# Dynamic convolution and a two-way maxout layer on one core: a new order of the 1024 inner units, a load in longer rows, and one softmax step in another place

## The chip, the cores and the metric

The kernel runs on one core of one Trainium2 chip. The metric is the device time of one execution in microseconds (us). A core has a matrix engine (TensorE, PE in the profile, with its weight loads shown apart as PEld), a vector engine (VectorE, DVE), an activation engine (ScalarE, ACT), a general engine (GpSimd, POOL) that in this kernel mostly issues DMAs, and SyncE (SP), which only issues DMAs. Each engine takes its own instructions in order and waits where one of them needs what another engine or a DMA has not yet finished.

## What is computed

Two layers follow each other, cut here to what matters:

```python
# x: [8, 4160, 192], weight_gen: [8, 4160, 8 heads, 7 taps]
w = softmax(weight_gen, over the 7 taps)
y[b, s, h, g] = sum over k of w[b, s, h, k] * x_padded[b, s + k, h, g]   # 6 zero rows in front of each sequence
# y as 33280 rows of 192; w1, w2: [192, 1024], w_out: [1024, 192]
out = maximum(y @ w1, y @ w2) @ w_out
```

The order of the 1024 inner units does not matter to the result, as long as the columns of `w1` and `w2` and the rows of `w_out` are taken in the same order.

## The kernel before, in words

The 33280 rows lie on 128 partitions, 260 consecutive rows on each; a "column" is one row on every partition. Columns are handled in 17 batches of 16 (the last has 4). Batches 0 and 1 are cut into units of 4 columns, the later ones into units of 8: units 0 to 7, then 8 to 36. Columns 32 to 39 are unit 8, the first half of batch 2.

**Convolution (DVE and ACT).** For each batch ACT takes the exponentials (`exp_sum`, L135), DVE sums them over the taps (`red`, L147), ACT takes the logarithm (`ln`, L151), DVE subtracts it (`shift`, L156), and `weights` (L159 to L170) lets ACT write the softmax weights twice each in bf16 to `en_t`. `mul` (L182) multiplies the 7 taps on DVE, and `adds` (L198, L204, L207) sums them to `y_t`. From unit 8 on, a DMA transpose issued by SP (L216) brings `y_t` to the feature layout `yt`. For units 0 to 7, PE does the sum of the taps and the transposition at once (`sum_transpose`, L239 to L257): it multiplies the products by an identity matrix into a PSUM tile `yps`, and ACT copies that to `yt` (L255, "feature copy" below).

**Inner layer (PE and ACT).** The maximum is written as `y@w1 + relu(y@(w2 - w1))`. So the kernel keeps `wd = w2 - w1` for the inner products (`hid_tile`, L291 to L304, PSUM tiles `hdp` and later `hd`), ACT takes the ReLU to `rd_t` (`relu`, L309), and the product `w10 = w1 @ w_out` is computed once on the chip (L594 to L667), so that an output is `yt @ w10` (`out_first`, L351) plus `rd_t @ wo` (`out_hidden`, L339). The 1024 inner units are cut into 8 chunks of 128; `wo` has the rows of one chunk on the 128 partitions, so that chunk f lies at `wo[:, f*192:(f+1)*192]`. `evac` (L378 to L413) lets ACT copy finished outputs from the PSUM tile `op_ps` to `o_t` (L395, "eviction" below), and SP stores them (L407).

**Weights at the start.** `load_w` and its neighbours (L537 to L552) bring `w1` and `w2` as f32 to the staging tiles `ws0E`, `ws1E` (rows 0 to 127) and `ws0T`, `ws1T` (rows 128 to 191, each half of the columns on 64 partitions). ACT casts `w1` to bf16 in three copies of 512 columns (L578, L632, L633). `w_diff` (L579 to L589) is called twice: the first call subtracts on DVE (L582, then L587) and copies three pieces to other partitions on ACT; the second subtracts once (L582) and copies on DVE. `wo` comes by one DMA from POOL (L621), behind two loads of `x` and ahead of a third, with f32 in HBM and bf16 in SBUF.

**Order.** The order on each engine is that of the code; nothing is rescheduled. The first part (L512 to L693) is written out by hand: the transposition of unit 0, first inner products, `w_diff(1)`, and so on. From group 3 on (`GROUPS`, two columns of work each up to column 15, then three) `hidden` (L458 to L485) puts the steps of a group in order: inner products, `out_first`, ReLU, `relay` (an ACT no-operation that waits for `out_first` and that `out_second` waits for), the last inner products, the last ReLU, then `ahead`, then `out_second` with `evac`, then `between`, then `beside`. Dictionary `early` (L712) gives `between` for groups 3 to 7, and the call at L785 gives `ahead` for groups 4 and 5: `weights(2, 0)`, the softmax weights of columns 32 to 39, is in `ahead` of group 5. `op_ps` and `yps` share a ring of two PSUM buffers up to group 7, so that `op_ps` of group 6 takes the buffer of `op_ps` of group 5 once its eviction is done.

Of the kernel before, what the change touches and what calls it, by code (L numbers as in the profile page):

```python
# [13 lines left out]
ALU = mybir.AluOpType  # L14
# [3 lines left out]
def _sub(base: bass.AP, off: int, dims):  # L18
    ap = [list(base.ap[0])] + [[int(s), int(c)] for s, c in dims]
    return dataclasses.replace(base, offset=base.offset + off, ap=ap)  # L20
# [3 lines left out]
def kernel(  # L24
# [9 lines left out]
    nc = tc.nc  # L34

    B, S, D = x.shape
    H, K = weight_gen.shape[2], weight_gen.shape[3]
    F = moe_w1.shape[1]
    P = 128
    PAD = K - 1  # L40
    WGC = H * K
    FCH = F // P
    HF = F // 2
# [10 lines left out]
    def pieces(b):  # L54
        n = BATCHES[b][1]
        at, done = [], 0
        for w in (4, 4, 4, 4) if b < 2 else (8, 8) if n == 16 else (n,):
            at.append((done, w))
            done += w
        return at  # L60
# [76 lines left out]
    def part(b, i, of):  # L137

        n = BATCHES[b][1]
        h0, h1 = n * i // of * H, n * (i + 1) // of * H  # L140
        return slice(h0, h1), h0 * K, [[K, h1 - h0], [1, K]]
# [7 lines left out]
    def ln(b, i=0, of=1):  # L149
        s_t = s_ts[b][:, part(b, i, of)[0]]  # L150
        nc.scalar.activation(out=s_t, in_=s_t, func=AF.Ln)  # L151
# [7 lines left out]
    def weights(b, o):  # L159

        w = dict(pieces(b))[o]
        if b not in en_ts:
            en_ts[b] = pen.tile([P, 16 * WGC * 2], BF16, name="en_t", tag="en")
        J = 2 if w == 4 and b < 2 else 1
        N = w * H // J
        for j in range(J):
            nc.scalar.activation(  # L167
                out=_sub(en_ts[b], (o * WGC + j * N * K) * 2, [[2 * N, K], [2, N], [1, 2]]),
                in_=_sub(wg_ts[b], (o * H + j * N) * K, [[1, K], [K, N], [0, 2]]), func=AF.Exp,
            )  # L170
# [62 lines left out]
    def half(j):  # L233
        return slice(64 * j, 64 * j + 64)


    LEFT = (0, 1, 2, K - 1)

    def sum_transpose(u, taps=range(K)):  # L239

        b, o, n = UNITS[u]
        assert n == 4
        yps = ps["r" if "r" in ps else "o"].tile([P, 1024], FP32, name="yps", tag="op")
        for k in range(6):
            for t in taps:
                for r in range(2):
                    at = (K * o + t * n) * D + k * P
                    nc.tensor.matmul(  # L248
                        yps[:, r * 512 + k * 64:r * 512 + (k + 1) * 64],
                        lhsT=m_t[half(r), at:at + P], rhs=ident[half(r), half(r)],  # L250
                        start=(k == 0 and t == taps[0]), stop=(t == taps[-1]),
                        skip_group_check=True,
                    )
        yt = pyt.tile([P, 8 // 2 * 3 * P], BF16, name="yt", tag="yt")
        yt_of[u] = nc.scalar.copy(out=_sub(yt, 0, [[64, 2], [P, 6], [1, 64]]),  # L255
                                  in_=_sub(yps, 0, [[512, 2], [64, 6], [1, 64]]))
        yt_ts[u] = yt  # L257
# [112 lines left out]
    def relay(last):  # L370

        go = nc.scalar.nop()  # L372
        for mm in last:
            tc.add_manual_dep(go.ins, mm.ins.name, SYNC, reason="bank of the other half")
        return go
# [50 lines left out]
    OUTS, c = [[], [], []], 0  # L426
# [8 lines left out]
    def room(g):  # L435

        t0, n = GROUPS[g]
        if "c" in ps:
            ab = ps["ab"].tile([P, 2048], FP32, name="hd2", tag="ab")
            for t in range(t0, t0 + n - 1):  # L440
                hd_at[t] = ab, (t - t0) * 1024
            hd_at[t0 + n - 1] = ps["c"].tile([P, 1024], FP32, name="hd1", tag="c"), 0
        else:
            for t in range(t0, t0 + n):
                hd_at[t] = ps["h"].tile([P, 1024], FP32, name="hdp", tag="hd"), 0
        rd = prd.tile([P, 3 * 1024], BF16, name="rd_t", tag="rd")
        for t in range(t0, t0 + n):
            rd_at[t] = (rd, t - t0)
        return rd

    def out_room(now, tag=None):
        tag = tag or ("r" if "r" in ps else "o")
        w, name = {"ab": (2048, "ab"), "c": (1024, "c")}.get(tag, (1024, "op"))
        tile_ = ps[tag].tile([P, w], FP32, name="op_ps", tag=name)
        for c in now:
            op_at[c // 2] = tile_, (c - now[0]) // 2 * D

    def hidden(g, now=(), between=lambda: None, beside=lambda: None, ahead=lambda: None):  # L458


        t0, n = GROUPS[g]
        rd = room(g)
        for t in range(t0, t0 + n - 1):
            hid_tile(t)
        if now:
            out_room(now, "ab" if n == 1 and "ab" in ps else None)
            last = out_first(now)
        if len(now) > 2:
            relu(rd, t0, n - 1)
        else:  # L470
            for t in range(t0, t0 + n - 1):
                relu(rd, t, 1)
        if now:
            go = relay(last)
        hid_tile(t0 + n - 1)
        if len(now) > 2:
            beside()
        relu(rd, t0 + n - 1, 1)
        ahead()
        if now:  # L480
            out_second(now, go)
            evac(now[0] // 2, len(now) // 2)
        between()
        if len(now) <= 2:
            beside()  # L485
# [17 lines left out]
    wd = consts.tile([P, 3 * F], BF16, name="wd")  # L503
    wo = consts.tile([P, FCH * D], BF16, name="wo")
# [7 lines left out]
    with tc.tile_pool(name="pstage", bufs=1) as pstage:  # L512
        ident_f = pstage.tile([P, P], FP32, name="ident_f")
        xs = pstage.tile([P, (PAD + 8) * D], FP32, name="xs")
        ws = {(kind, wi): pstage.tile([P, w], FP32, name=f"ws{wi}{kind}")
              for kind, w in (("E", F), ("T", HF)) for wi in range(2)}
# [3 lines left out]
        for p0, p1 in ((1, 16), (16, P)):  # L520
            nc.sync.dma_start(
                out=xs[p0:p1, 0:PAD * D],
                in_=bass.AP(tensor=x.tensor, offset=(p0 * CPP - PAD) * D,
                            ap=[[CPP * D, p1 - p0], [1, PAD * D]]),
# [20 lines left out]
        for wi, wsrc in enumerate((moe_w1, moe_w2)):  # L545
            for h in range(2):
                nc.sync.dma_start(
                    out=ws["T", wi][half(h), :],
                    in_=bass.AP(tensor=wsrc.tensor, offset=P * F + h * HF, ap=[[F, 64], [1, HF]]),
# [20 lines left out]
        for o in (0, 4, 8, 12):  # L570
            weights(0, o)
        nc.vector.tensor_copy(out=xb_ts[0][:, PAD * D:(PAD + 4) * D],
                              in_=xs[:, PAD * D:(PAD + 4) * D])
        first_mul = mul(0, 0)
        w1 = {kind: pstage.tile([P, w], BF16, name="w1" + kind)
              for kind, w in (("E", F), ("T", HF))}

        nc.scalar.copy(out=w1["E"][:, 0:HF], in_=ws["E", 0][:, 0:HF])  # L578
        def w_diff(h, copy):  # L579

            c0 = slice(h * HF, (h + 1) * HF)
            nc.vector.tensor_tensor(out=wd[:, c0], in0=ws["E", 1][:, c0], in1=ws["E", 0][:, c0],  # L582
                                    op=ALU.subtract)
            copy(out=wd_at(1, 2, h, 0, HF), in_=wd[0:64, c0])
            copy(out=wd_at(0, 1, h, 0, HF), in_=wd[64:P, c0])
            if h == 0:
                nc.vector.tensor_tensor(out=wd[:, 2 * HF:3 * HF], in0=ws["T", 1], in1=ws["T", 0],  # L587
                                        op=ALU.subtract)
            copy(out=wd_at(1 - h, 1 + h, h, 0, HF), in_=wd[half(h), 2 * HF:3 * HF])  # L589


# [18 lines left out]
        def keep_warm(times):  # L610
# [8 lines left out]
        behind(first_mul, load_x(0, 8, 4))  # L619
        load_x(0, 12, 4)  # L620
        nc.gpsimd.dma_start(  # L621
            out=wo[:, :].rearrange("p (f d) -> p f d", d=D),
            in_=bass.AP(tensor=moe_w_out.tensor, offset=0, ap=[[D, P], [P * D, FCH], [1, D]]),
        )
        load_x(1, 0, 8)

# [2 lines left out]
        mul(0, 4)  # L629


        nc.scalar.copy(out=w1["T"], in_=ws["T", 0])  # L632
        nc.scalar.copy(out=w1["E"][:, HF:F], in_=ws["E", 0][:, HF:F])  # L633
        rd = room(0)
        hid_tile(0)
        relu(rd, 0, 1)
# [65 lines left out]
    def end_of_1():  # L702
# [8 lines left out]
    none = lambda: None  # L711
    early = {  # L712
        3: (none, rest_of_1),
        4: (lambda: (behind(relu_of[8], load_x(2, 0, 8, halo=False)), sum_transpose(4),
                     behind(yt_of[4], load_wg(4, nc.gpsimd))), end_of_1),
        5: (lambda: sum_transpose(5, LEFT), none),
        6: (lambda: (behind(relu_of[12], load_x(2, 8, 8)), weights(2, 8), ln(3), sum_transpose(6, LEFT)), none),
        7: (lambda: (behind(relu_of[14], load_x(3, 0, 8)), sum_transpose(7, LEFT)), none),
    }
# [60 lines left out]
    for g in range(4, len(GROUPS)):  # L780
        if GROUPS[g][1] == 3 and "c" not in ps:
            later_ps()
        tiles = [t for t in range(GROUPS[g][0], sum(GROUPS[g])) if t >= 16]
        if g in early:
            hidden(g, OUTS[g], early[g][0], ahead=lambda: {4: lambda: (weights(1, 12), ln(2)), 5: lambda: weights(2, 0)}.get(g, none)())  # L785
            early[g][1]()
            steps(g, tiles)
        else:
            hidden(g, OUTS[g], beside=lambda: steps(g, tiles))
# [30 lines left out]
```

## Time and profile before

| | |
|---|---|
| median of 5 runs | 411.57 us (411.0 to 413.79) |
| the profiled execution, its own time | 412.04 us |
| its span, first to last instruction | 410.3 us |
| granted TensorE clock in it | 0.999 |
| busy PE, DVE, ACT, POOL | 398.4, 374.7, 357.5, 73.3 us |
| DMA traffic | 65.68 MB, mean 160 GB/s |
| load of `wo`: 384 KB, issue to landing | 7.8 us |

The page gives each engine's busy time, then the span in 40 slices, the DMA queues, the chain of work that ended last (followed back from the last instruction to what released it), and the costliest groups of instructions. The timeline gives the instructions of an engine in order: start, duration, engine, line, operation, and in brackets the idle time before it and what ended that. [...]

### The profile page before, as it was taken

To read this page: it belongs to the slowest core of one execution; us is meant where nothing else is said; L and a number is where in the kernel's file an instruction comes from. 1 tells how busy PE (TensorE), PEld (TensorE's weight loads), DVE (VectorE), ACT (ScalarE), POOL (GpSimd) and SP (SyncE) were. 2 spreads that over 40 slices of the span, in tenths; PEclk is the share of its full clock that TensorE was granted. 3 is DMA by queue.
4 is the path that set the end of the run, shared out by engine and by line. 5 is a ranking of instruction groups with operands and counts; after the bars stand their busy time and mean duration, and the time that the engine had idled before them with its cause. 6 is when DMAs were issued, how large, how long until landed. Compare 5 with 4: busy or idle time off the path is not lost.

```text
span 410.3 us, 15992 instructions
## 1 busy us (share of the span) xinstructions
PE 398.4 (97%) x7350; PEld 317.0 (77%) x7350; DVE 374.7 (91%) x219; ACT 357.5 (87%) x424; POOL 73.3 (18%) x101
## 2 busy tenths in 40 slices
PE   7889999999999999999999999999999999999995
PEld 3679899677777877777787778777777777787795
DVE  5999999999999999999999999999999999999000
ACT  6898998989999998899988999988999989888771
POOL 0311103121211022222101222211122212110000
PEclk9999999999999999999999999999999999999999
DMA  8966577768667864974787497489548638744513
GB/s 240 237 145 182 101 147 160 182 150 180 147 104 209 207 137 98 257 165 88 215 174 174 92 252 186 74 201 241 112 103 244 166 59 248 150 89 69 223 61 136
DMA packets 60384, 65.68 MB, mean 160 GB/s; under 512 B 47615, under 2 KB 48511, under 8 KB 60318
## 3 DMA queue, kind: packets, MB, share of 16 engines
q1 hardware_dynamic: 51934, 40.54, 36.5%
q0 software_dynamic: 8240, 24.04, 29.3%
q8 instruction: 57, 0.93, 0.9%
q10 hardware_dynamic: 144, 0.10, 0.1%
q14 instruction: 9, 0.07, 0.1%
HBM read 35.96 MB, written 25.56 MB: 150 GB/s over the span
## 4 chain that ended last, share of the span: by engine, by line
PE 83%; ACT 11%; DMA 3%; issue 2%; DVE 0%; SPq 0%; ACTq 0%
PE op_ps L339 38%; PE hd L299 36%; PE op_ps L351 7%; ACT rd_t L309 6%; DMA xs<-in_x_dram 3%; ACT en_t L167 1%; PE hdp L299 1%; ACT o_t L395 1%; ACT yt L255 1%; ACT e_t L135 1%; PE yps L248 0%; PE pw L655 0%; ACT sum_t L151 0%; ACT w L666 0%; ACT wd L589 0%
## 5 line engine op out<-in xcount | busy, mean ns | idle before, releaser
L309 ACT ACTIVATE rd_t<-hd 128x1024 bf16<-128x1024 f32 (+1 forms) x206 | 234.6, 1189 | 27.7 <-PE hd L299 26.3
L339 PE MATMUL op_ps<-wo,rd_t 64*128 64x192 bf16 x4160 | 210.5, 243 | 0.1
L339 PEld LDWEIGHTS <-rd_t 64*128 64x128 bf16 x4160 | 180.8, 94 | 15.7 <-ACTq L372 0.3
L299 PE MATMUL hd<-yt,wd 64*128 64x512 bf16 (+1 forms) x1584 | 187.3, 360 | 1.2 <-ACT rd_t L309 1.2
L182 DVE TENSOR_TENSOR m_t<-xb_t,en_t 128x10752 bf16<-128x10752 bf16 (+1 forms) x37 | 187.5, 5071 | 0.4
L299 PEld LDWEIGHTS <-wd 64*128 64x128 bf16 x1776 | 94.1, 94 | 43.2 <-issue 3.0
L224 POOL CAST gate<-yt 128x1 f32<-128x1 bf16 x29 | 38.6, 1332 | 272.0 <-DMA yt<-y_t 272.0
L198 DVE TENSOR_TENSOR m_t<-m_t 128x4608 bf16<-128x4608 bf16 (+1 forms) x32 | 76.8, 2401 | 0.1
L395 ACT COPY o_t<-op_ps 128x384 f32<-128x384 f32 (+1 forms) x99 | 57.3, 591 | 14.0 <-PE op_ps L339 13.3
L351 PE MATMUL op_ps<-w,yt 64*128 64x192 bf16 x780 | 55.5, 243 | 1.0 <-ACT o_t L395 1.0
L351 PEld LDWEIGHTS <-yt 64*128 64x128 bf16 x780 | 38.4, 94 | 17.5 <-issue 2.1
L204 DVE TENSOR_TENSOR m_t<-m_t 128x3072 bf16<-128x3072 bf16 (+1 forms) x29 | 50.0, 1724 | 0.1
L167 ACT ACTIVATE en_t<-wg_t 128x896 bf16<-128x896 f32 (+2 forms) x45 | 35.4, 821 | 0.0
L207 DVE TENSOR_TENSOR y_t<-m_t 128x1536 bf16<-128x1536 bf16 (+1 forms) x29 | 27.3, 941 | 0.5
L385 DVE COPY o_last<-op_ps 128x192 f32<-128x192 f32 x1 | 0.4, 357 | 26.1 <-ACT o_last L385 26.1
L156 DVE TENSOR_TENSOR wg_t<-wg_t,sum_t 128x280 f32<-128x280 f32 (+5 forms) x46 | 22.1, 481 | 0.2
L147 DVE TENSOR_REDUCE sum_t<-e_t 128x64 f32<-128x448 f32 (+2 forms) x31 | 19.6, 635 | 2.6 <-ACT e_t L135 2.6
L114 POOL DMA_DIRECT2D xb_t<-in_x_dram x33 | 17.7, 535 | 22.9 <-ACT rd_t L309 11.9
L135 ACT ACTIVATE e_t<-wg_t 128x896 f32<-128x896 f32 (+2 forms) x18 | 16.1, 899 | 2.6 <-DMA wg_t<-in_weight_gen_dram 2.6
L309 ACT ACTIVATE rd_t<-hdp 128x1024 bf16<-128x1024 f32 x16 | 16.2, 1047 | 0.6 <-PE hdp L299 0.6
L299 PE MATMUL hdp<-yt,wd 64*128 64x256 bf16 x192 | 12.9, 269 | 0.2
L613 PE MATMUL warm<-ident 128*128 128x512 bf16 x38 | 10.5, 441 | 2.6 <-DVE ident L560 2.6
(46 smaller groups left out, 73.8 us busy)
## 6 DMA issues: line engine op xcount, KB each, us to landing
out_dram<-o_t SPq DMA_DIRECT2D x28, 768.0 KB, 4.9
xb_t<-in_x_dram POOLq DMA_DIRECT2D x30, 384.0 KB, 4.9
wg_t<-in_weight_gen_dram POOLq DMA_DIRECT2D x14, 448.0 KB, 5.4
xb_t<-xb_t POOLq DMA_DIRECT2D x16, 288.0 KB, 5.3
out_dram<-o_t SPq DMA_DIRECT2D x8, 384.0 KB, 4.2
wg_t<-in_weight_gen_dram SPq DMA_DIRECT2D x2, 448.0 KB, 4.5
xs<-in_x_dram SPq DMA_DIRECT2D x2, 384.0 KB, 6.4
xb_t<-in_x_dram POOLq DMA_DIRECT2D x3, 192.0 KB, 4.5
```

The source lines that it names most:

```text
L156: nc.vector.tensor_tensor(out=w_t, in0=w_t, in1=_sub(s_ts[b], hs.start, [[1, hs.stop - hs.start], [0, K]]), op=ALU.subtract)
L167: nc.scalar.activation(out=_sub(en_ts[b], (o * WGC + j * N * K) * 2, [[2 * N, K], [2, N], [1, 2]]), in_=_sub(wg_ts[b], (o * H + j * N) * K ...
L182: return nc.vector.tensor_tensor(out=m_out, in0=x_in, in1=_sub(en_ts[b], o * WGC * 2, [[2, K * n * H], [0, G // 2], [1, 2]]), op=ALU.mult,)
L198: nc.vector.tensor_tensor(out=taps(0, 1, 3), in0=taps(0, 1, 3), in1=taps(3, 1, 3), op=ALU.add)
L204: nc.vector.tensor_tensor(out=taps(0, 2, 2), in0=taps(0, 2, 2), in1=taps(1, 5, 2), op=ALU.add)
L207: nc.vector.tensor_tensor(out=_sub(y_ts[b], o * D, [[64, 2], [P, 3 * w // 2], [1, 64]]), in0=taps(0, 1, 1), in1=taps(2, 1, 1), op=ALU.add,)
L224: nc.gpsimd.tensor_copy(out=gate, in_=yt[:, 0:1])
L299: nc.tensor.matmul(hid_out(t, f, j), lhsT=wd_at(j, s, f // 4, f % 4 * P, P), rhs=_sub(yt_ts[u][half(j), :], (s + j) % 3 * P, [[3 * P, w // ...
L309: relu_of[t0] = nc.scalar.activation(out=rd[:, k * 1024:(k + n) * 1024], in_=hd[:, at:at + n * 1024], func=AF.Relu)
L339: return nc.tensor.matmul(op_out(c), lhsT=rd[half(r), k * 1024 + at:k * 1024 + at + P], rhs=wo[half(r), f * D:(f + 1) * D], start=False, s ...
L351: nc.tensor.matmul(op_out(c + j), lhsT=yt_ts[u][half(j), (3 * i + (s + j) % 3) * P:(3 * i + (s + j) % 3 + 1) * P], rhs=w10[half(j), s * D: ...
L395: nc.scalar.copy(out=_sub(o, c % 24 * D, [[D, len(qs)], [h * D, 2], [1, D]]), in_=_sub(tile_, at + (qs[0] - p) * D, [[D, len(qs)], [512, 2 ...
```

## The change

The chunks of inner units are taken differently. Before, partition p of chunk c in half h held unit 512h + 128c + p. After, it holds unit 512h + 4p + c, so that the four rows of `w_out` that partition p needs for a half lie behind each other in HBM. The load of `wo` becomes 128 x 2 rows of 768 elements (3072 bytes) where it was 128 x 8 rows of 192 elements (768 bytes). To match, the three subtractions and the three casts read the f32 staging tiles with a step of four elements (16 bytes) between neighbours (`spread`) and write chunk after chunk (`by_chunk`); the written tiles, the partition copies and everything that PE reads keep their layout.

Second, `weights(2, 0)` moves from `ahead` of group 5 to `between` of the same group: on ACT it now comes after the eviction of group 5 and the feature copy of unit 5, and before the first ReLU of group 6. On the other engines the order of instructions is unchanged.

```diff
-        nc.scalar.copy(out=w1["E"][:, 0:HF], in_=ws["E", 0][:, 0:HF])
+        def spread(t, c0):
+
+            return _sub(t, c0, [[1, 4], [4, P]])
+
+        def by_chunk(t, c0):
+
+            return _sub(t, c0, [[P, 4], [1, P]])
+
+        nc.scalar.copy(out=by_chunk(w1["E"], 0), in_=spread(ws["E", 0], 0))
         def w_diff(h, copy):
 
             c0 = slice(h * HF, (h + 1) * HF)
-            nc.vector.tensor_tensor(out=wd[:, c0], in0=ws["E", 1][:, c0], in1=ws["E", 0][:, c0],
-                                    op=ALU.subtract)
+            nc.vector.tensor_tensor(out=by_chunk(wd, h * HF), in0=spread(ws["E", 1], h * HF),
+                                    in1=spread(ws["E", 0], h * HF), op=ALU.subtract)
             copy(out=wd_at(1, 2, h, 0, HF), in_=wd[0:64, c0])
             copy(out=wd_at(0, 1, h, 0, HF), in_=wd[64:P, c0])
             if h == 0:
-                nc.vector.tensor_tensor(out=wd[:, 2 * HF:3 * HF], in0=ws["T", 1], in1=ws["T", 0],
-                                        op=ALU.subtract)
+                nc.vector.tensor_tensor(out=by_chunk(wd, 2 * HF), in0=spread(ws["T", 1], 0),
+                                        in1=spread(ws["T", 0], 0), op=ALU.subtract)
...
         nc.gpsimd.dma_start(
-            out=wo[:, :].rearrange("p (f d) -> p f d", d=D),
-            in_=bass.AP(tensor=moe_w_out.tensor, offset=0, ap=[[D, P], [P * D, FCH], [1, D]]),
+            out=wo[:, :].rearrange("p (h e) -> p h e", h=2),
+            in_=bass.AP(tensor=moe_w_out.tensor, offset=0, ap=[[4 * D, P], [HF * D, 2], [1, 4 * D]]),
         )
...
-        nc.scalar.copy(out=w1["T"], in_=ws["T", 0])
-        nc.scalar.copy(out=w1["E"][:, HF:F], in_=ws["E", 0][:, HF:F])
+        nc.scalar.copy(out=by_chunk(w1["T"], 0), in_=spread(ws["T", 0], 0))
+        nc.scalar.copy(out=by_chunk(w1["E"], HF), in_=spread(ws["E", 0], HF))
...
-        5: (lambda: sum_transpose(5, LEFT), none),
+        5: (lambda: (sum_transpose(5, LEFT), weights(2, 0)), none),
...
-            hidden(g, OUTS[g], early[g][0], ahead=lambda: {4: lambda: (weights(1, 12), ln(2)), 5: lambda: weights(2, 0)}.get(g, none)())
+            hidden(g, OUTS[g], early[g][0], ahead=lambda: {4: lambda: (weights(1, 12), ln(2))}.get(g, none)())
```

## The prediction, as it was made before the changed kernel had run

> **What bounds the kernel now.** I read the page first: busy time by engine, then the 40 slices, then the chain.
>
> ```profile
> PE 398.4 (97%) x7350; PEld 317.0 (77%) x7350; DVE 374.7 (91%) x219; ACT 357.5 (87%) x424; POOL 73.3 (18%) x101
> PE   7889999999999999999999999999999999999995
> ACT  6898998989999998899988999988999989888771
> PE 83%; ACT 11%; DMA 3%; issue 2%; DVE 0%; SPq 0%; ACTq 0%
> ```
>
> The second and third lines are the slices, the fourth the chain by engine. From about 50 us on PE is full to the end, so a time lost or won before that is kept: PE has a fixed amount of work left. The change touches only the start, where ACT is as full as PE. So the view that decides is the chain, piece by piece (start, length, what), in the first 50 us.
>
> ```profile
> 13.28 0.58 DVE xb_t L618
> ...
> 13.87 0.62 ACT wd L589
> ...
> 14.51 0.80 ACT yt L255
> 15.31 0.52 ACT w1T L632
> 15.83 0.52 ACT w1E L633
> 16.35 0.92 ACT rd_t L309
> ...
> 22.43 0.97 PE yps L248 x57
> ...
> 25.99 1.44 PE pw L655 x16
> ...
> 40.67 0.90 ACT en_t L167
> 41.57 0.38 ACT o_t L395
> ...
> 41.99 0.42 PE op_ps L351 x6
> ```
>
> Two of the three casts that now read with a step (L632, L633) are pieces of the chain, and the third edit's step (L167 at 40.67) is one too. The load of `wo` is in no piece. In the timeline ACT's first partition copy (L584, at 12.60) waited 1.88 us for the first subtraction, L582, so that one is ahead of this chain too.
>
> **Part 1, the load of `wo`.** Removed: 1024 rows of 768 bytes; added: 256 rows of 3072. POOL issues it at 13.45 in 0.92 us and it lands 7.8 us after, at 21.25. Its first reader is L655 at 25.92, 4.7 us later, and that one is ordered behind the copies of `w1t` on ACT (end 24.97). So a faster load releases nobody. The x loads of the same queue have rows of this length: two of them issued at 12.27 in 1.20 us, 0.60 each, and landed in 4.5 (median). As an estimate `wo` lands up to 3 us sooner and POOL's next load, columns 0 to 7 of batch 1, is issued 0.3 sooner. That one is needed by the `mul` at 26.2 on DVE, and the copy of its six leading columns, issued at 18.28 and landing in 5.3, by 23.6. That is a cover of 2.6 us. Were the load slower by any amount below 4.7 nothing would be late either. I cost it at 0; the cover is the time up to 25.92. What else shorter traffic could give is PE's own instruction supply ("issue" 0.71 at 23.40 and 0.49 before 28.91): an upper bound of 1.2 us of gain. I take 0 of it, because both stalls fall after `wo` has landed.
>
> **Part 2, the reads with a step.** Same instruction count. The trace has no f32 read of SBUF with 16 bytes between neighbours that are each read once, so I bound the price. Nearest rows (count, busy, mean ns, idle):
>
> ```profile
> L135 ACT ACTIVATE e_t<-wg_t 128x896 f32<-128x896 f32 x4 | 3.9, 964 | 0.0
> L167 ACT ACTIVATE en_t<-wg_t 128x896 bf16<-128x896 f32 x2 | 2.1, 1042 | 0.0
> L582 DVE TENSOR_TENSOR wd<-ws1E,ws0E 128x512 bf16<-128x512 f32 x2 | 1.4, 684 | 0.0
> L156 DVE TENSOR_TENSOR wg_t<-wg_t,sum_t 128x448 f32<-128x448 f32 x2 | 1.2, 617 | 0.0
> ```
>
> Lower end: L167 reads f32 with 28 bytes between neighbours, each one twice, and takes 1042 ns where the plain L135 takes 964: 8%, which is nothing here (0.05 us a cast). It could not be below zero, since no element is saved. Upper end: a rate halved, as one element per access could do. The rate on DVE comes from L156 in two sizes: 1085 ns for 896 and 617 for 448, so 1.045 ns an element; halved, 512 elements cost d = 0.535 us more on top of 684 ns. That rates move by a factor of two is in the trace: `mul` does 10752 bf16 in 5.75 us, 0.535 ns an element. On ACT, L135 in two sizes (964 for 896, 568 for 448) gives 0.884 ns an element, so a = 0.45 us more on top of 0.62.
>
> I take the upper end for both engines, by the same row of L167 counted otherwise. Its 896 elements are only 448 different addresses. L167 in two sizes (1042 ns for 448 addresses, 410 for 112) costs 1.88 ns for each further address, about twice the 0.884 of L135. If the cost goes by addresses and not by elements, it is the halved rate. Which of the two counts is meant, no row tells; this is a choice.
>
> [...]
>
> Now the path. ACT: the first cast (L578 at 10.10) ends a later, in the 1.88 us of idle, and costs nothing. L582 ends d later, so L584, L585 and, behind L587 at 13.21 + 2d = 14.28, L589 (13.87 + d = 14.41) all move by d. The feature copy moves by d, L632 and L633 add a each: the ReLU at 16.35 starts at 16.35 + d + 2a = 17.79. PE's inner products for it start at 15.36 + d and take 0.8, so they are ready by 16.7. The ACT chain is therefore 1.435 us late (0.535 + 0.90).
>
> DVE: L582 and L587 add 2d, of which 0.07 was a wait for the x rows before 13.28; the second L582 adds d: 3d - 0.07 = 1.535 us late at L147 (18.38). Its exponentials are ready at 18.11 + 1.435 = 19.55, before 19.92. The `mul` that ends at 22.25 ends at 23.79; the transposition on PE that needs it started at 22.43 and can start at 22.43 + 1.435 = 23.87. So DVE stays just behind the cover, and the path's price is ACT's 1.435. Later on everything on the path is released by something that has moved as much: the product at 25.99, the copies of `w10`, the ReLUs.
>
> Does DVE's 1.535 come back at the end? DVE has no idle time after 13.28, and the tightest feature tile I found lands at 356.99 (gate copy of POOL) for an inner product at 357.48: 0.49 us of slack. PE being about 1.2 late itself, DVE at 1.535 uses 0.3 of it. Nothing is added.
>
> **Part 3, the moved softmax step.**
>
> ```profile
> 40.53 1.05 ACT L167 ACTIVATE en_t<-wg_t 128x896 bf16<-128x896 f32 x1
> 41.43 0.51 ACT L395 COPY o_t<-op_ps 128x384 f32<-128x384 f32 x1
> 41.79 0.85 ACT L255 CAST yt<-yps 128x768 bf16<-128x768 f32 x1
> 42.48 1.09 ACT L309 ACTIVATE rd_t<-hdp 128x1024 bf16<-128x1024 f32 x1
> 43.77 1.02 ACT L309 ACTIVATE rd_t<-hdp 128x1024 bf16<-128x1024 f32 x1 [0.20 <-PE hdp L299]
> ```
>
> PE waits 0.81 us at 41.99 for that eviction, since the next group's outputs need its buffer. Moved behind, the softmax step lets the eviction run at 40.67 to 41.05 (its outputs ended near 39.8), and PE's outputs start at 41.1. But 0.81 is not the gain. ACT does the same four steps before the ReLU, 0.38 + 0.70 + 0.90 + 0.92, and ends that ReLU at 43.57 as before. The ACT no-operation behind it releases PE's second half of outputs, so these still start near 43.6 (43.55 before). What is won is ACT's wait of 0.20 at 43.77: PE's last inner products of the group end near 42.85 rather than 43.75, so the second ReLU follows at 43.57. ACT stays full to 48.8 and PE's next stage (48.86) waits for ACT, so the 0.20 is kept. Behind the moved step stands only that ReLU; its reader, the `mul` at 44.62 on DVE, finds the weights written at about 42.65. Gain: 0.20 us; bounds 0 and 0.81.
>
> **Sum.** 1.435 + 0 - 0.20 = +1.235 us on the profiled execution: 412.04 becomes 413.3. That execution is 0.47 above the median of the runs, 411.57, and medians are what will be compared, so I predict 411.57 + 1.235 = 412.8. That is 0.3% more. A measurement of this kernel can tell about 0.5%, 2.06 us, from no change, so this counts as the same.
>
> **Rivals.**
>
> *A, forecast: reads at half rate on both engines,* 412.8. Chance 0.50. Against it: no row shows it.
>
> *B, reads with a step are free.* For it: L167's 8%. Then only -0.20 is left: 411.4. It includes the case that the longer rows of `wo` do just what they say and nobody waits for them. One engine alone paying lies between: DVE alone gives d = 0.535 by ACT's chain, but 1.535 - 0.18 by DVE's cover (22.25 against 22.43), so +1.16 after the 0.20; ACT alone gives 0.90 - 0.20 = +0.70. Together 0.30.
>
> *C, slower: the subtractions pay for both of their operands.* DVE reads two tiles with a step, ACT one. If the two reads share the penalty, d doubles to 1.07 with a = 0.45. DVE is then 3.14 late and the `mul` ends at 25.39, past PE's 22.43 + 1.97: the transposition of unit 2 waits for DVE, and PE is 2.96 late from there. It decides from d > a + 0.125, that is 0.575. With -0.20 it gives 411.57 + 2.76 = 414.3, slower by 0.67%. Chance 0.15.
>
> *D, faster:* PE's two instruction stalls of 1.2 us go with the lighter traffic, and the reads are free: 411.57 - 1.4 = 410.2. For it: both are near loads; against it: `wo` has landed before both. Chance 0.05, and it is inside 0.5%.
>
> **Numbers.** Range: from B less the 0.5 us that single runs lie below the median, 410.9, to C's 414.3. Faster by over 0.5% needs 2.06 us; only D goes that way, and only with a third stall on top (later ones of 0.7 and 1.4 us are in the chain at 76.30 and 187.06): 0.04. Slower by over 0.5%: C's 0.15 and a little of A with a late release on top, 0.19. Same: 0.77.
>
> **What would show it.** Right: the rows of the two L582 and of L587 rise from 684 and 693 to about 1220 ns, those of the casts from 622 to about 1070; the first ReLU starts near 17.8; PE's wait of 0.81 for the eviction of group 5 is gone and the wait of 0.20 ahead of the ReLU with it, while the second outputs still start right behind a ReLU. `wo` lands sooner and L655 doesn't wait for it before or after. Wrong: rows of 0.7 us (B); rows of DVE near 1.75 us with PE waiting for `mul` at L248 (C); a wait of PE on feature tiles near 357 us, which would mean that DVE's slack of 0.49 was too small.

## The result, and the profile after

| | before | after |
|---|---|---|
| median of all runs | 411.3 us (95 runs, 410.43 to 414.29) | 412.25 us (53 runs, 411.40 to 413.73) |
| ratio after/before | | 1.0015, 95% interval 1.0008 to 1.0022 |
| span of the profiled execution | 410.3 us | 410.6 us |
| load of `wo`, issue to landing | 7.8 us | 7.5 us |
| PE's wait for the eviction of group 5 | 0.81 us | none |

The change costs 0.15%, about 0.6 us (interval 0.3 to 0.9), where +1.235 us was forecast. The times of both kernels spread by 2 to 4 us, and the kernel before has more high ones, so the measure matters: the means differ by 0.62 us, as the ratio has it, the medians by 0.95, the lowest times by 0.97.

Busy time and the chain by engine, after:

```profile
PE 399.3 (97%) x7350; PEld 317.2 (77%) x7350; DVE 375.7 (91%) x219; ACT 358.7 (87%) x424; POOL 67.7 (16%) x101
PE 51%; DVE 28%; ACT 13%; DMA 3%; issue 3%; SPq 1%; DVEq 0%; ACTq 0%
```

The busy times of PE, DVE and ACT rose by about 1 us each. The chain moved much more: DVE, which had 0% of it, has 28%. 28% of the span is 115 us along which the chain runs through DVE and no longer through PE.

The changed instructions, from the groups of the first 60 us (count, busy us, mean ns, idle before):

```profile
L590 DVE TENSOR_TENSOR wd<-ws1E,ws0E 128x512 bf16<-128x512 f32 x2 | 2.2, 1086 | 0.0
L595 DVE TENSOR_TENSOR wd<-ws1T,ws0T 128x512 bf16<-128x512 f32 x1 | 1.1, 1083 | 0.0
L640 ACT CAST w1T<-ws0T 128x512 bf16<-128x512 f32 x1 | 1.1, 1137 | 0.0
L641 ACT CAST w1E<-ws0E 128x512 bf16<-128x512 f32 x1 | 1.1, 1117 | 0.0
```

A subtraction on DVE went from 684 to 1086 ns (+0.40 us), a cast on ACT from 622 to 1117 and 1137 (+0.50). The chain of the first 50 us after (start, length, what; in the timelines, rows that follow each other on DVE, ACT and PE overlap by up to about 0.1 us, and the chain counts only the rest, so that the cast of 1137 ns is 1.03 there):

```profile
14.25 0.62 ACT wd L597
14.89 0.80 ACT yt L255
15.69 1.03 ACT w1T L640
16.72 1.02 ACT w1E L641
17.74 0.92 ACT rd_t L309
...
33.21 0.65 PE hdp L299 x12
...
35.47 1.02 ACT rd_t L309
...
41.02 0.37 ACT o_t L395
41.39 0.70 ACT yt L255
42.09 0.49 ACT en_t L167
42.58 0.30 issue
42.88 1.97 ACT rd_t L309 x2
```

Lay it beside the chain before. The first ReLU is at 17.74 instead of 16.35, late by 1.39. But the ReLU at 35.47 was at 35.11: only 0.36 is left. The two ReLUs at 42.88 now follow each other without a wait, and PE enters its full stage at 48.92 where it did at 48.86. PE's wait for the eviction of group 5, before and after:

```profile
41.99 0.42 PE L351 MATMUL op_ps<-w,yt 64*128 64x192 bf16 x6 [0.81 <-ACT o_t L395]
```

```profile
41.45 0.42 PE L351 MATMUL op_ps<-w,yt 64*128 64x192 bf16 x6
```

Nearly all the loss at the start is gone by 50 us. So two questions arise: where did 1.0 us go between 18 and 35 us, and where does the end come from, if not from there?

**Where 1.0 us went.** PE's rows from 22 to 30 us, before and then after (the bracket is the idle time before the row):

```profile
22.39 1.02 PE L248 MATMUL yps<-ident,m_t 64*128 64x64 bf16 x57
24.11 0.56 PE L248 MATMUL yps<-ident,m_t 64*128 64x64 bf16 x27 [0.71 <-issue]
...
27.35 1.07 PE L248 MATMUL yps<-ident,m_t 64*128 64x64 bf16 x61
28.91 0.52 PE L248 MATMUL yps<-ident,m_t 64*128 64x64 bf16 x23 [0.49 <-issue]
```

```profile
23.63 1.00 PE L248 MATMUL yps<-ident,m_t 64*128 64x64 bf16 x57
24.89 0.56 PE L248 MATMUL yps<-ident,m_t 64*128 64x64 bf16 x27 [0.25 <-issue]
...
28.12 1.40 PE L248 MATMUL yps<-ident,m_t 64*128 64x64 bf16 x84
```

Before, PE stops in the middle of a row of like matmuls, at number 57, with nothing to wait for but "issue". After, PE comes 1.24 us later to the same place and stops only 0.25 us; the second stop is gone. Counted over loads and matmuls, the stops lie at PE's instructions 705 and 961, 256 apart. The trace has an instruction queue (`q8 instruction: 57, 0.93 MB` on the page before) that moves 16384 bytes at a time, a block: before, such transfers ended at 22.72 and 27.63, and PE went on 1.38 and 1.28 us later, at 24.11 and 28.91. The reading is that PE waits there for its own program, and that whoever comes later finds it there. PE was 1.24 us late ahead of the two places and is 0.37 late behind them (29.62 against 29.25).

**Where the end comes from.** The feature tile of unit 31 near 335 us, before and then after (POOL's "gate" row starts 0.12 us after the tile has landed, at 334.64 and 334.99):

```profile
334.68 0.82 PE L299 MATMUL hd<-yt,wd 64*128 64x512 bf16 x6
334.76 0.43 POOL L224 CAST gate<-yt 128x1 f32<-128x1 bf16 x1 [10.77 <-DMA yt<-y_t]
```

```profile
335.03 0.82 PE L299 MATMUL hd<-yt,wd 64*128 64x512 bf16 x6 [0.25 <-DMA yt<-y_t]
335.11 0.30 POOL L224 CAST gate<-yt 128x1 f32<-128x1 bf16 x1 [10.54 <-DMA yt<-y_t]
```

Before, the tile landed when PE wanted it. After, PE waits for it, and from there on every PE row is 0.35 us late instead of 0.06. DVE made that tile 0.58 us later than before (its lateness was 1.0 us from 33 us on; 0.4 of it went at 168.84 and 240.03, where DVE before had a short wait for ACT's logarithm), and its transposition landed 5.14 us after issue instead of 5.37. The 0.35 is, but for 0.02, the difference of the spans.

The traces also show something about why this tile has no slack. In the kernel before, its transposition takes 5.37 us to land and that of unit 30 takes 3.67. A 16384-byte transfer of the instruction queue (332.57 to 333.46) runs wholly during the first; during the second, issued at 317.42, one runs only for its first 0.22 us (316.58 to 317.64). Over all 14 profiles of this case, the 101 transpositions without such a transfer landed in 3.63 to 4.62 us (median 3.68) and the 305 with one in 3.64 to 5.67 (median 4.00); unit 31's always had one. That the transfer holds the tile up was not tested.

### The profile page after: what moved, and what is told of

Read it like the earlier page. It is cut to its first block, busy times and chain, and to the rows that moved or that the text cites. A ratio compares the mean times of both kernels' runs of the same rounds, so it can differ in the third digit from the quotient of the medians.

```text
span 410.6 us, 15992 instructions
## 1 busy us (share of the span) xinstructions
PE 399.3 (97%) x7350; PEld 317.2 (77%) x7350; DVE 375.7 (91%) x219; ACT 358.7 (87%) x424; POOL 67.7 (16%) x101
## 4 chain that ended last, share of the span: by engine, by line
PE 51%; DVE 28%; ACT 13%; DMA 3%; issue 3%; SPq 1%; DVEq 0%; ACTq 0%
PE op_ps L339 24%; PE hd L299 23%; DVE m_t L182 14%; ACT rd_t L309 8%; DVE m_t L198 6%; PE op_ps L351 4%; DVE m_t L204 4%; DMA ws1T<-in_moe_w_dram 2%; DVE y_t L207 1%; ACT en_t L167 1%; DVE sum_t L147 1%; DMA yt<-y_t 1%; DVE wg_t L156 1%; ACT o_t L395 1%; ACT yt L255 1%
## 5 line engine op out<-in xcount | busy, mean ns | idle before, releaser
L224 POOL CAST gate<-yt 128x1 f32<-128x1 bf16 x29 | 33.1, 1140 | 276.6 <-DMA yt<-y_t 276.6
L156 DVE TENSOR_TENSOR wg_t<-wg_t,sum_t 128x280 f32<-128x280 f32 (+5 forms) x46 | 22.1, 481 | 0.0
```

The costliest lines, as they stand in the source:

```text
L156: nc.vector.tensor_tensor(out=w_t, in0=w_t, in1=_sub(s_ts[b], hs.start, [[1, hs.stop - hs.start], [0, K]]), op=ALU.subtract)
L224: nc.gpsimd.tensor_copy(out=gate, in_=yt[:, 0:1])
```

## The experiments

The theory drawn from the two traces: the reads with a step make ACT and DVE late at the start; ACT's lateness is mostly swallowed by PE's stops for instructions, and DVE's goes on until a feature tile without slack hands it to PE. In the expectations it is theory 1 or A. Its rivals are the prediction's account, in which the start's lateness is kept and DVE has cover (theory 2 or B), the traffic of the load (theory 3), and, for PE's stops, whether that traffic makes them (C) or not (D).

There are three kinds of runs: parts of the change alone, one engine made late by added work, and attempts to take the two limits away. Ratios are against the kernel before; "lowest" is to be set beside that of the kernel before in the same comparison, which has 30 to 35 runs against 12 (7 for one) and so a better chance of a low one. The difference of the medians is not that of the ratio: in wo_late the median is 0.44 us lower at a ratio of 1.0000. Differences below about half a us are not to be relied on.

| run | ratio (95%) | median | lowest | before: median, lowest |
|---|---|---|---|---|
| only_move | 1.0010 (0.9986 to 1.0033) | 412.07 | 410.54 | 411.36, 410.42 |
| only_order | 1.0018 (1.0003 to 1.0033) | 412.40 | 411.94 | 411.36, 410.42 |
| plain_reads | 0.9990 (0.9970 to 1.0010) | 411.36 | 410.50 | 411.36, 410.42 |
| old_load | 1.0012 (0.9993 to 1.0031) | 412.18 | 411.63 | 411.36, 410.42 |
| act_late | 1.0015 (1.0003 to 1.0028) | 412.22 | 411.61 | 411.63, 410.78 |
| dve_late | 1.0020 (1.0003 to 1.0037) | 412.80 | 411.50 | 411.63, 410.78 |
| after_one_shift | 1.0041 (1.0020 to 1.0062) | 413.90 | 412.85 | 411.63, 410.78 |
| move_one_shift | 1.0023 (1.0002 to 1.0043) | 412.42 | 411.29 | 411.63, 410.78 |
| dve_strided | 1.0017 (0.9998 to 1.0037) | 412.73 | 412.16 | 411.82, 410.46 |
| act_strided | 1.0008 (0.9990 to 1.0026) | 412.15 | 411.67 | 411.82, 410.46 |
| wo_late | 1.0000 (0.9989 to 1.0011) | 411.38 | 410.79 | 411.82, 410.46 |
| wo_late_move | 0.9990 (0.9974 to 1.0005) | 411.47 | 410.25 | 411.82, 410.46 |

### The parts alone

**only_move**, against the kernel before:

```diff
-        5: (lambda: sum_transpose(5, LEFT), none),
+        5: (lambda: (sum_transpose(5, LEFT), weights(2, 0)), none),
...
-            hidden(g, OUTS[g], early[g][0], ahead=lambda: {4: lambda: (weights(1, 12), ln(2)), 5: lambda: weights(2, 0)}.get(g, none)())
+            hidden(g, OUTS[g], early[g][0], ahead=lambda: {4: lambda: (weights(1, 12), ln(2))}.get(g, none)())
```

> The kernel before with only the softmax step moved; rows read plainly, old load. Theory 1 (the changed kernel's end is set by VectorE's lateness reaching TensorE at a late feature tile; what ScalarE and TensorE lose at the start is mostly taken up by TensorE's waits for its own instructions): TensorE enters its full stage near 48.6 instead of 48.9, but VectorE is as before, so the tile of unit 31 (landing at 334.8 with no slack) gives the gain back: 0.0 us, between -0.2 and +0.1. Theory 2 (the prediction's: what TensorE wins at the start is kept): -0.2 us.

In time: inconclusive, the interval holds both. In the trace, theory 1's early gain was not seen either: PE entered its full stage 0.84 us later than in the kernel before, since this execution had the two stops, of 1.15 and 1.04 us, and a third of 0.41 at 38.84. What the move alone does ahead of 50 us is read better from the other runs, as PE's lateness against the kernel before at 32 us and at 50 us: with the move -1.03 and -1.33 (plain_reads), -0.01 and -0.31 (old_load), +0.36 and +0.06 (after); without it +0.10 and +0.11 (only_order). So it wins 0.30 us there.

**only_order**, against the changed kernel: the same two lines set back.

> The changed kernel with the softmax step back in its old place; the new order of the inner units, the reads with a step and the load in longer rows stay. Theory 1: ScalarE and TensorE enter the full stage 0.3 to 0.4 us late (the moved step no longer gives 0.3 back), VectorE about 1.0 us late; the end about +0.4 to +0.7 us over the kernel before, so the same as the changed kernel or up to 0.2 more. Theory 2: +1.4 us over the kernel before.

+0.7 us by the ratio, as theory 1 has it, and +1.04 by the medians, between the two; theory 2's +1.4 lies at the very end of the interval. This favours theory 1 and does not settle it. The first ReLU on ACT was late as in the changed kernel (5.64 us after PE's first transposition in both, 4.23 in the kernel before), and PE entered its full stage 0.11 us late, less than theory 1's 0.3 to 0.4. Taking the move out costs no time that can be told.

**plain_reads**, against the changed kernel:

```diff
-            return _sub(t, c0, [[1, 4], [4, P]])
+            return _sub(t, c0, [[P, 4], [1, P]])
```

> The changed kernel with the six casts and subtractions reading neighbours again (the inner units of w1 and w2 are then paired with the wrong rows of w_out, which leaves all work in place). Theory 1: the subtractions fall from 1086 to about 684 ns, the casts from 1104 to 1137 to about 622 ns, VectorE is on time again, and the time is that of the kernel before or up to 0.2 us below it. Theory 3 (the load in longer rows changes the traffic and with it the landings of feature tiles): the 0.6 us stay without the reads with a step.

```profile
L590 DVE TENSOR_TENSOR wd<-ws1E,ws0E 128x512 bf16<-128x512 f32 x2 | 1.4, 684 | 0.0
L641 ACT CAST w1E<-ws0E 128x512 bf16<-128x512 f32 x1 | 0.6, 621 | 0.0
```

The rows are back at 684 and 621 ns, and the median is that of the kernel before (411.36), with the longer rows of the load still in; in the same comparison old_load and only_order, which keep the reads with a step, are at 412.18 and 412.40. So the reads with a step are the loss. Theory 3 fell: its 0.6 us lie above the interval, which ends at +0.4.

**old_load**, against the changed kernel:

```diff
-            out=wo[:, :].rearrange("p (h e) -> p h e", h=2),
-            in_=bass.AP(tensor=moe_w_out.tensor, offset=0, ap=[[4 * D, P], [HF * D, 2], [1, 4 * D]]),
+            out=wo[:, :].rearrange("p (f d) -> p f d", d=D),
+            in_=bass.AP(tensor=moe_w_out.tensor, offset=0, ap=[[D, P], [P * D, FCH], [1, D]]),
```

> The changed kernel with the load of the output weights in 1024 short rows again (wrong pairing of the inner units, all work in place). Theory 1: time as in the changed kernel, +0.6 us over the kernel before, since nobody waits for that load; its landing goes back to about 7.8 us. Theory 3: the time goes back towards the kernel before, or rises by over 0.3 us if the longer rows had won something.

+0.12% with 1024 short rows, beside +0.15% with 256 long ones: no difference that can be told. The load landed in 7.2 us here, in 6.3 to 7.5 with long rows (only_order, plain_reads, after_one_shift, after) and in 7.0 to 8.4 with short ones elsewhere when issued as early (in 5.2 when issued at 18.77, in wo_late): the longer rows win well under 1 us of landing, and nobody waits for it.

### One engine late on purpose

**act_late**, against the kernel before:

```diff
         nc.scalar.copy(out=w1["T"], in_=ws["T", 0])
+        nc.scalar.copy(out=w1["T"], in_=ws["T", 0])
+        nc.scalar.copy(out=w1["T"], in_=ws["T", 0])
```

> The kernel before, with the cast of w1's last 64 rows (L632) done three times: ScalarE 1.04 us later from 15.8 us on, VectorE untouched; nothing of the result changes. Theory A (TensorE stalls at a fixed place of its program, instruction 705, until a block of instructions has come, and a later TensorE finds the block there): the stall of 0.9 us before L248 near 23 us shrinks or is gone, the lowest time rises by 0.7 to 1.0 us, the median by 0.2 to 0.6 only. Theory B (the prediction's: the lateness is kept): lowest time and median both rise by 1.0 us.

PE's rows from 22 to 29 us of this run:

```profile
22.97 1.47 PE L248 MATMUL yps<-ident,m_t 64*128 64x64 bf16 x84
...
27.14 1.40 PE L248 MATMUL yps<-ident,m_t 64*128 64x64 bf16 x84
```

All 84 in one row, twice: both stops are gone. The two added casts made ACT 1.31 us later, not 1.04: from the start of the first cast of this tile to the first ReLU it is 2.35 us (14.62 to 16.97), 1.04 in the kernel before (15.21 to 16.25). The lowest time rose by 0.83 and the median by 0.59 us, as theory A said. All of the 1.31 kept would be 0.32%, above the interval's end at 0.28; theory B's 1.0 us by itself is inside it.

One profile could miss the stops by chance. Four profiles have the same program up to 30 us (before, only_move, move_one_shift, dve_late): at instruction 705 they stop for 0.71, 1.15, 0.94 and 0 us, at 961 for 0.49, 1.04, 0.22 and 0. The five with a late ACT (after, only_order, old_load, after_one_shift, act_late) stop for 0.25 us at 705 in one and not at all in the others. So the stops differ from execution to execution, and a late ACT mostly does away with them. It would follow that the kernel before has its low times when it has no stops, and that a later ACT takes those away; that was not shown.

**dve_late**, against the kernel before (the repeated sum writes the same tile):

```diff
-    def red(b, i=0, of=1):
-        if i == 0:
+    def red(b, i=0, of=1, again=False):
+        if i == 0 and not again:
...
         red(2)
+        red(2, again=True)
         adds(1, 4, True)
```

> The kernel before, with the sum over the taps of batch 2 (L147 near 32 us) done twice: VectorE 1.0 us later from 33 us on, ScalarE and TensorE untouched until 50 us; nothing of the result changes. Theory A (VectorE's lateness reaches the end by itself, where TensorE waits for the feature tile of unit 31 near 335 us, which had no slack): +0.3 to +0.8 us, with TensorE's step of that size at unit 31. Theory B (VectorE has cover to the end): 0.0 us.

```profile
312.05 0.82 PE L299 MATMUL hd<-yt,wd 64*128 64x512 bf16 x6 [0.99 <-DMA yt<-y_t]
312.13 0.58 POOL L224 CAST gate<-yt 128x1 f32<-128x1 bf16 x1 [10.26 <-DMA yt<-y_t]
```

PE, 0.21 us early until then, waits 0.99 us for the tile of unit 29. The time rose by 0.2%, 0.8 us. So 1.0 us of DVE alone, put where ACT and PE do not feel it, costs about what the whole change costs, and theory B, the prediction's reckoning of cover, fell. The trace shows the way but not the size: in this execution loads came late as well, DVE was already 0.9 us late at 32.96, where the doubled sum begins, and 2.0 us late from 46 us on. And of the 2.7 us by which the tile of unit 29 landed later, DVE made 1.54; the rest is its transposition, which took 4.86 us to land where it took 3.69 before.

**dve_strided** and **act_strided**, against the kernel before, have the strided form in only the three subtractions (first hunk), or only the three casts (second hunk); one of each is shown:

```diff
-            nc.vector.tensor_tensor(out=wd[:, c0], in0=ws["E", 1][:, c0], in1=ws["E", 0][:, c0],
-                                    op=ALU.subtract)
+            nc.vector.tensor_tensor(out=by_chunk(wd, h * HF), in0=spread(ws["E", 1], h * HF),
+                                    in1=spread(ws["E", 0], h * HF),
+                                    op=ALU.subtract)
...
-        nc.scalar.copy(out=w1["E"][:, 0:HF], in_=ws["E", 0][:, 0:HF])
+        nc.scalar.copy(out=by_chunk(w1["E"], 0), in_=spread(ws["E", 0], 0))
```

> The kernel before, where only the three subtractions on VectorE read with the step of 16 bytes (ScalarE's casts and the load plain, so the inner units of wd and w1 are paired wrongly; all work in place). Theory A (two ways to the end: TensorE late at the start, in part hidden by its waits for instructions; VectorE late at the feature tiles near 310 to 335 us): VectorE about 1.1 us late from 20 us on and to the end, ScalarE 0.4 us late at its first ReLU; median +0.4 to +0.9 us over the kernel before. Theory B (only the ScalarE way of the prediction counts): +0.4 us or less after what the waits take, lowest time +0.4.

> The kernel before, where only ScalarE's three casts read with the step (wrong pairing again, all work in place). Theory A: as with the two extra casts, the first ReLU 1.0 us late, no stall before instruction 705 of TensorE, lowest time +0.6 to +0.9, median +0.3 to +0.7 us over the kernel before. Theory B: lowest and median +1.0 us.

Each half alone costs something at the low end (lowest +1.7 and +1.2 us). The medians rose by 0.9 and 0.3 us, and neither interval excludes 1 by itself, so whether the halves add up to the whole (0.95 by the medians) can't be told. In the profile of dve_strided PE was 0.08 us early at 50 us and late by 0.75 after the tiles of units 29 and 31 (waits of 0.48 and 0.12 us): VectorE's way, as theory A has it. That of act_strided began with x rows that came late (its first transposition on PE 1.05 us later than in the kernel before), so its trace tells nothing of ACT's way, and its time does not tell theory A from B.

### Taking the limits away

**after_one_shift** and **move_one_shift**: the changed kernel, and only_move, with

```diff
-            adds(c, 0, beside=lambda i, of: shift(c + 1, i, of) if c + 1 < NB else None)
+            adds(c, 0, beside=lambda i, of: shift(c + 1) if c + 1 < NB and i == 0 else None)
```

> The changed kernel, with the subtraction of the logarithms (L156) in one instruction a batch where it was three: about 0.13 us of VectorE saved in each of 13 batches, 1.5 us or more by unit 31. Theory A: TensorE no longer waits for the tile of unit 31 (0.29 us in the profiled execution of the changed kernel), and the time falls by 0.2 to 0.6 us against the changed kernel, to +0.1 to +0.4 over the kernel before. Theory B: VectorE is off the path, the time is that of the changed kernel, +0.6 over the kernel before.

> The kernel before (plain reads, old load) with the moved softmax step and the subtraction of the logarithms in one instruction a batch. Theory A: the 0.3 us that the move wins ahead of 50 us are no longer taken back at unit 31: 0.3 to 0.6 us below the kernel before, the fastest of all. Theory B: 0.2 us below, as the move alone would be.

Both missed, the other way: DVE got slower. One batch of after_one_shift on DVE, and PE at unit 29 in it:

```profile
75.83 1.08 DVE L156 TENSOR_TENSOR wg_t<-wg_t,sum_t 128x896 f32<-128x896 f32 x1
76.83 2.55 DVE L198 TENSOR_TENSOR m_t<-m_t 128x4608 bf16<-128x4608 bf16 x1
79.42 1.76 DVE L204 TENSOR_TENSOR m_t<-m_t 128x3072 bf16<-128x3072 bf16 x1
81.21 0.96 DVE L207 TENSOR_TENSOR y_t<-m_t 128x1536 bf16<-128x1536 bf16 x1
82.09 5.75 DVE L182 TENSOR_TENSOR m_t<-xb_t,en_t 128x10752 bf16<-128x10752 bf16 x1
```

```profile
313.15 0.82 PE L299 MATMUL hd<-yt,wd 64*128 64x512 bf16 x6 [1.03 <-DMA yt<-y_t]
313.23 0.48 POOL L224 CAST gate<-yt 128x1 f32<-128x1 bf16 x1 [10.36 <-DMA yt<-y_t]
```

From L156 to the next `mul` it is 6.26 us; with three pieces it was 6.15 (73.95 to 80.10 in the kernel before). An addition that reads what the one before wrote starts 0.03 to 0.04 us after its end, while a piece of the subtraction put between starts about 0.1 before it. What the merging saves, these two bubbles take and more. Between 62 us and unit 31 DVE fell behind the kernel before by a further 0.78 us in both runs, where the changed kernel caught up 0.42, and the time went up: here too DVE's lateness arrives at the end as PE's wait for a feature tile.

**wo_late** and **wo_late_move**: the kernel before, and only_move, with the load of `wo` issued behind the next one:

```diff
+        load_x(1, 0, 8)
         nc.gpsimd.dma_start(
             out=wo[:, :].rearrange("p (f d) -> p f d", d=D),
             in_=bass.AP(tensor=moe_w_out.tensor, offset=0, ap=[[D, P], [P * D, FCH], [1, D]]),
         )
-        load_x(1, 0, 8)
```

> The kernel before, with the load of the output weights issued behind the next load of x and its copy of leading columns, so at about 18.8 instead of 13.45 us; it lands near 25 us, about when its first reader wants it. Theory C (the block of instructions that TensorE lacks at instruction 705 comes late because its transfer queues behind the traffic of this load): the transfer of that block starts by 21 us and the stall is gone in the profile; median 0.3 to 0.7 us below the kernel before, times less spread. Theory D (the traffic of this load has no part in it): median as before within 0.2 us, or later by up to 0.5 us where the load comes too late for L655.

> The same as the run with the late load, with the softmax step moved as in the changed kernel. Theory C: 0.1 to 0.3 us below that run, the best of all, at 410.6 to 411.0. Theory D: as the move alone, no gain that can be told.

In wo_late the transfer of the block that PE lacked at 705, by the reading above, began at 18.19 us instead of 21.78, in wo_late_move at 19.78, and neither had the stop. That is theory C's sign, and in the 12 profiles with an early load it began later, at 20.18 to 22.74. But plain_reads, dve_late and others lack the stop too, with an early load. The highest of 12 times was 412.22 and 412.35, where the kernel before reached 415.05 in 35: less spread, as theory C said, but in two runs only. The ratios are 1.0000 and 0.9990, and the intervals hold 1. No version was shown to beat the kernel before.

## Why the prediction was right, and where it was not

The time lies in its range, and "the same within 0.5%" was right. That says little of the mechanism: the range of 410.9 to 414.3 also holds the 411.3 of the kernel before. The forecast of +1.235 us was about twice the +0.6 measured by the ratio (1.3 times the 0.95 of the medians). By its steps:

- **The price of a read with a step.** Right in kind: the chosen upper end and not the lower. d was 0.40 us where 0.535 was reckoned, a was 0.50 where 0.45 was. With 16 bytes between neighbours, a subtraction on DVE took 1.6 times as long (1086 against 684 ns) and a cast on ACT 1.8 times (1117 and 1137 against 622). "As one element per access could do" was the author's estimate; no run shows what sets the price. plain_reads shows that these reads are the cause.
- **The first stretch of the path.** Right in the path; that 1.435 us reckoned for the first ReLU met the 1.39 measured is in part luck, since d was 0.13 too large and 2a 0.10 too small. DVE was reckoned 1.535 late and was 1.0 to 1.16 late.
- **"I take 0 of it", of PE's two stops, and "everything on the path is released by something that has moved as much".** This step failed. The block transfers did not wait for ACT (the first began at 20.62 to 22.21 in the four profiles with the program of before, at 20.18 to 22.74 in the five with a late ACT), so the stops shrank by 0.95 us (0.71 to 0.25 and 0.49 to none), and PE's lateness with them from 1.24 to 0.37. act_late shows it with the delay alone. The bound of 1.2 us was put on the wrong side: the stops were no gain for the load to make, but a cushion for every delay ahead of them, and only in executions that have them.
- **DVE's cover, "the tightest feature tile I found lands at 356.99".** This step failed. The tile of unit 31 lands, by the same gate copy, at 334.76 for a row of PE at 334.68, with no slack. The reckoning took one late tile for the tightest; all 29 have to be looked up. "DVE has no idle time after 13.28" was not right either: its two short waits gave 0.4 us back. In the profiled execution 0.29 of the 0.35 us come from this tile; dve_late and after_one_shift show the way by itself. The sign of being wrong that was named, a wait of PE on a feature tile near 357 us, came at 335.
- **The moved step, -0.20.** The mechanism was right (the 0.81 becomes no gain, ACT's wait goes); the size was 0.30. One sign was missed: the second outputs did not start behind that ReLU but at 43.01, while it ran (42.88 on), straight behind PE's own inner products; it cost nothing, since PE's next stage waits for ACT. At the end no gain could be told.
- **The load, 0.** Right for the path; the landing of "up to 3 us sooner" was far too much, 0.3 us in the profiled execution.
- **The rivals.** B fell with the rows of 1.1 us; C fell because DVE paid 0.40, under its point of 0.575. D's sign, fewer stops, appeared without its gain, because PE came later.

What stays open: how much of the 0.6 us is ACT's way and how much DVE's. act_late and dve_late show that lateness of either engine alone costs time, and the intervals are too wide to divide the loss between them. What sets the moment at which a block transfer begins is open too: the first of the two began from 18.19 to 22.74 us in these traces. So is whether these transfers also hold up the feature tiles that they meet.

## What to carry to other kernels

Here a layout change that made one load longer-rowed was paid by the engines that then read the staged data with a step (0.40 us a subtraction and 0.50 a cast, for a load that landed 0.3 us sooner); price both, and first ask whether anybody waits for the load. Slack of a late engine must be looked up at every hand-over, not at a few: here the one tile without slack decided. And the waits that the profile calls "issue" swallowed most of a delay here (PE was 1.24 us late ahead of them and 0.37 behind), while with one and the same program the first of these waits was 0.71, 1.15, 0.94 and 0 us, so the part of a delay that they swallow can differ from execution to execution: compare lowest times and medians, not two profiles.

## What the runs showed of the hardware that was not expected

- PE stops, as if for its own instructions, at places that are multiples of 256 apart in its program (705 and 961, in one run 1473, in another 449), until about 1.2 to 1.45 us after the end of a 16384-byte transfer of the instruction queue. The stop at 705 was 0.71, 1.15, 0.94 and 0.25 us in four kernels' profiles and absent in the other ten.
- A DMA transposition to a feature tile landed 3.63 to 4.62 us after its issue when no such transfer ran meanwhile (101 of 406, median 3.68 us) and up to 5.67 us when one did.
- In the rows shown, an addition on DVE that reads the result of the one before starts 0.03 to 0.04 us after its end; an instruction that does not starts about 0.1 us before the end of its predecessor. Small independent work between dependent instructions cost less than the same work in one piece: 6.15 against 6.26 us a batch.
